# Depthwise convolution and token mixer: DMA transposes against TensorE transposes with packed matmul tiles and a static schedule

## Chip, cores and metric

The kernel runs on one core of a Trainium2 chip. The metric is the device time of one execution in microseconds (us); smaller is better. In this text PE is TensorE, DVE is VectorE, ACT is ScalarE, POOL is GpSimd and SP is SyncE. A matmul has a stationary operand, which a weight load (PEld) brings into PE, and a moving operand. The time from the start of one matmul to the start of the next grows with the columns of the moving operand (192 columns 83 ns, 512 columns 216 ns in the trace of before, so 2.4 columns per ns); that time is called streaming here. The programs write the results to PSUM, which they use in banks. To evacuate a result is to copy it out of PSUM with DVE or ACT. Two small stationary operands can share the array (in the trace of after both of such a pair start 0 to 5 ns apart): side by side they are called column tiles here, one above the other row tiles. A landing is the end of a DMA transfer.

## The reference, cut to what matters

```python
# x: (8, 4224, 192) float32; weight: (8, 7); w_q, w_k: (192, 64); w_out: (192, 192)
w = softmax(weight)                       # one 7-tap filter for each of 8 heads of 24 channels
x = causal_conv(x, w)                     # out[s] = sum_k w[k] * x[s - 6 + k], per channel
wq = x @ w_q;  wk = x @ w_k
W_tok = (1 / 8) * einsum('bsd,btd->bst', wq, wk)
mixed = einsum('bst,btd->bsd', W_tok, x)
out = maximum(mixed, 0) @ w_out           # (8, 4224, 192) float32
```

No softmax stands between the two products, so both kernels reorder them. They form the Gram matrix G = xᵀx of the convolved x once per batch and compute `relu(x @ (scale * w_q w_kᵀ G)) @ w_out`. A convolution over 128 tokens is a product with a 128×128 band matrix, of which 122 outputs are valid. Both programs make G from x with tokens on the partitions and run the second pass on x with channels on the partitions, so one of the two forms is made by transposing.

## The kernel before

The convolution puts channels on the partitions, with 24-column tiles of the array. DVE copies the result to `XT`. SyncE then transposes it with the DMA engines to `XS`, in five pieces per batch and two transposes per piece, and the Gram products run when all of it has landed.

```python
# gen_conv_block: four chunks of 122 tokens, four heads side by side in the array
last = te.matmul(
    tile[32 * g : 32 * g + GRP, CW * ci : CW * ci + ncol],
    XW[0:kc, xbuf, c, GRP * h : GRP * h + GRP],
    BAND[0:kc, h, 0:ncol],
    start=True, stop=True,
    tile_position=(0, 32 * g),
)
# ... DVE: XT <- tile ...
# gen_transpose_piece
for t in range(2):
    sy.dma_start_transpose(
        XS[:, xbuf, i0 : i0 + nchunk, 128 * t : 128 * t + 128],
        XT[:, xbuf, t, s0 : s0 + plen],
    ).then_inc(ch.sem, 16)
# gen_g_chunk: 33 chunks a batch, 2 x 256 columns each
te.matmul(P_G0[:, 0:256], XS[:, xbuf, i, 0:128], xall, start=first, stop=last)
mm = te.matmul(P_G1[:, 0:256], XS[:, xbuf, i, 128:256], xall, start=first, stop=last)
# ... M = wkᵀ G, A = wq M (192 x 192) ...
# gen_mx_quad: four 128x128 matmuls of 512 columns
last = te.matmul(P_MX[m][:, 0:ncols], A_SB[:, tt, 128 * m : 128 * m + 128],
                 XT[:, xbuf, tt, s0 : s0 + ncols], start=(tt == 0), stop=(tt == 1))
# ... ACT: RT <- relu; gen_final: two matmuls of 192 columns per 128 tokens ...
# stores from POOL: a row of 192 floats (768 bytes) per token
dst = bass.AP(out_t, (b * S + jstart * 128) * D, [[D, 128], [128 * D, nsubs], [1, D]])
```

Of the kernel before, what the change touches and what calls it, by code (L numbers as in the profile page):

```python
# [9 lines left out]
F32 = mybir.dt.float32  # L10


def bass_lightweight_conv__then__hypermixer_token_mlp_kernel(
# [12 lines left out]
    assert S % 128 == 0 and S >= 1024  # L26
    assert D == 192 and H == 8 and KC == 7 and DH == 64 and GRP == 24

    x_t = x.tensor
    out_t = out.tensor  # L30
    w_t = weight.tensor
    wq_t = moe_w_q.tensor
    wk_t = moe_w_k.tensor
    wo_t = moe_w_out.tensor

    CW = 122
    NCC = (S + CW - 1) // CW
    NBLOCK = (NCC + 3) // 4
    NQT = (S + 511) // 512
    NSUB = S // 128  # L40
    NCH = S // 128
    PIECES = []
    c0 = 0
    for size in (8, 8, 8, 6, 100):
        if c0 >= NCH:
            break
        PIECES.append(list(range(c0, min(c0 + size, NCH))))
        c0 += size
    NPIECE = len(PIECES)
    scale = 1.0 / (float(DH) ** 0.5)  # L50

    es = contextlib.ExitStack()
    es.__enter__()

# [3 lines left out]
    def psum(name):  # L58
        return es.enter_context(nc.psum_tensor(name, [128, 512], F32))

    class Chan:
        def __init__(self, name):
            self.sem = es.enter_context(nc.semaphore(name))
            self.v = 0

        def inc(self, n=1):
            self.v += n
            return self.v

    c_wsetup = Chan("c_wsetup")  # L70
    c_xload = [[Chan(f"c_xl{xb}_{i}") for i in range(3)] for xb in range(2)]
    c_spdma = Chan("c_spdma")
    c_tp = [[Chan(f"c_tp{xb}_{p}") for p in range(NPIECE)] for xb in range(2)]
    c_odma = [Chan("c_odma0"), Chan("c_odma1")]
    c_dve = Chan("c_dve")
    c_act = Chan("c_act")
    c_gp = Chan("c_gp")
    c_convA = Chan("c_convA")
    c_convB = Chan("c_convB")
    c_evA = Chan("c_evA")  # L80
    c_evB = Chan("c_evB")
    c_gd = Chan("c_gd")
    c_ge = Chan("c_ge")
    c_md = Chan("c_md")
    c_me = Chan("c_me")
    c_ad = Chan("c_ad")
    c_ae = Chan("c_ae")
    c_mxd = Chan("c_mxd")
    c_mxe = Chan("c_mxe")
    c_fd = Chan("c_fd")  # L90
    c_fe = [Chan("c_fe_dve"), Chan("c_fe_act")]

    WT_F = sbuf("wt_f", [128, H * KC], F32)
    WMX = sbuf("wmx", [128, H], F32)
    WEX = sbuf("wex", [128, H, KC], F32)
    WSM = sbuf("wsm", [128, H], F32)
    WSOFT = sbuf("wsoft", [128, H, KC], F32)
    DMASK = sbuf("dmask", [128, KC, 128], F32)
    BANDF = sbuf("bandf", [128, 128], F32)
    BAND = sbuf("band", [128, H, 128], BF16)  # L100
    IDENT_T = sbuf("ident_t", [128, 128], F32)
    IDENT = sbuf("ident", [128, 128], BF16)
    WQP = sbuf("wqp", [128, 2, DH], BF16)
    WQT = sbuf("wqt", [DH, 2, 128], BF16)
    WKP = sbuf("wkp", [128, 2, DH], BF16)
    WOP = sbuf("wop", [128, 2, D], BF16)
    XW = sbuf("xw", [128, 2, NCC, D], BF16)
    XT = sbuf("xt", [128, 2, 2, S], BF16)
    XS = sbuf("xs", [128, 2, NCH, 256], BF16)
    G_SB = sbuf("g_sb", [128, 2, 256], BF16)  # L110
    M_SB = sbuf("m_sb", [DH, 256], BF16)
    A_SB = sbuf("a_sb", [128, 2, 256], BF16)
    RT = sbuf("rt", [128, 2, 2, 512], BF16)
    OUT_SB = sbuf("out_sb", [128, 2, 8, D], F32)

    P_CONVA = psum("p_conva")
    P_CONVB = psum("p_convb")
    P_G0 = psum("p_g0")
    P_G1 = psum("p_g1")
    P_M = psum("p_m")  # L120
    P_MX0 = psum("p_mx0")
    P_MX1 = psum("p_mx1")
    P_A = psum("p_a")
    P_OUTS = [P_G0, P_G1]
    P_MX = [P_MX0, P_MX1]

    conv_mm_ch = [c_convA, c_convB]
    conv_ev_ch = [c_evA, c_evB]
    conv_tile = [P_CONVA, P_CONVB]

    streams = {"pe": [], "act": [], "dve": [], "sp": [], "pool": []}

    def pe(f):
        streams["pe"].append(f)

    def act(f):
        streams["act"].append(f)

    def dve(f):
        streams["dve"].append(f)  # L140

    def sp(f):
        streams["sp"].append(f)

    def pool(f):
        streams["pool"].append(f)

    def waiter(eng, waits):
        for s, v in waits:
            if v > 0:  # L150
                eng.wait_ge(s, v)

    def _setup_sp(sy):
        src = bass.AP(w_t, 0, [[0, 128], [1, H * KC]])
        sy.dma_start(WT_F[:, :], src).then_inc(c_spdma.sem, 16)

    sp(_setup_sp)
    v_wtf = c_spdma.inc(16)

    def _setup_pool_mem(gp):  # L160
        gp.memset(WQP[:, :, :], 0.0).then_inc(c_gp.sem, 1)
        gp.memset(WKP[:, :, :], 0.0).then_inc(c_gp.sem, 1)
        gp.memset(WOP[:, :, :], 0.0).then_inc(c_gp.sem, 1)
        gp.memset(XW[0:6, :, 0, :], 0.0).then_inc(c_gp.sem, 1)

    pool(_setup_pool_mem)
    v_gp_mem = c_gp.inc(4)

    def _setup_pool_dma(gp, v_mem=v_gp_mem):
        gp.wait_ge(c_gp.sem, v_mem)  # L170
        for t in range(2):
            for g in range(4):
                d0 = 96 * t + 24 * g
                gp.dma_start(
                    WQP[32 * g : 32 * g + 24, t, :],
                    bass.AP(wq_t, d0 * DH, [[DH, 24], [1, DH]]),
                ).then_inc(c_wsetup.sem, 16)
                gp.dma_start(
                    WKP[32 * g : 32 * g + 24, t, :],
                    bass.AP(wk_t, d0 * DH, [[DH, 24], [1, DH]]),  # L180
                ).then_inc(c_wsetup.sem, 16)
                gp.dma_start(
                    WOP[32 * g : 32 * g + 24, t, :],
                    bass.AP(wo_t, d0 * D, [[D, 24], [1, D]]),
                ).then_inc(c_wsetup.sem, 16)

    v_wload = None

    v_mx = c_dve.inc(1)
    v_sub = c_dve.inc(H)  # L190

    def _setup_dve_softmax(ve, v_wtf=v_wtf, v_mx=v_mx):
        wt3 = WT_F[:, :].rearrange("p (h k) -> p h k", k=KC)
        ve.wait_ge(c_spdma.sem, v_wtf)
        ve.tensor_reduce(WMX[:, :], wt3, AX.X, ALU.max).then_inc(c_dve.sem, 1)
        ve.wait_ge(c_dve.sem, v_mx)
        for h in range(H):
            ve.tensor_scalar(
                WEX[:, h, :], wt3[:, h, :], WMX[:, h : h + 1], None,
                op0=ALU.subtract,  # L200
            ).then_inc(c_dve.sem, 1)

    dve(_setup_dve_softmax)

    def _setup_act_exp(sc, v_sub=v_sub):
        sc.wait_ge(c_dve.sem, v_sub)
        sc.activation(WEX[:, :, :], WEX[:, :, :], AF.Exp).then_inc(c_act.sem, 1)

# [142 lines left out]
    def piece_chunks(p):  # L351
        return PIECES[p]

# [512 lines left out]
```

## Time and profile before

| | before |
|---|---|
| time, median of 3 runs | 378.26 us (377.14 to 381.84) |
| PE / DVE / ACT busy | 66% / 40% / 31% of the span |
| chain that ended last | PE 35%, DMA 23%, SyncE's queue 17% |

The page gives for each engine its busy time, and in its second part the busy share in 40 equal slices (each digit is tenths). "Chain that ended last" follows the last instruction back to what released it. From the page of the kernel before: PE's total, its slices, and the chain by engine and by line.

```profile
PE 247.1 (66%) x3618; PEld 158.0 (42%) x3618; DVE 149.5 (40%) x301; ACT 116.6 (31%) x244; POOL 84.7 (23%) x123
...
PE   0001447479586958796769868975789297959671
...
PE 35%; DMA 23%; SPq 17%; DVE 13%; issue 5%; ACT 5%; POOL 0%; DVEq 0%; POOLq 0%
SPq L479 17%; DMA xs<-xt 12%; PE p_mx L584 11%; DMA out_dram<-out_sb 10%; PE p_conva L437 6%; PE p_g L501 5%; DVE xt L460 5%; DVE bandf L281 5%; PE p_g L502 4%; PE p_g L622 3%; ACT rt L603 3%; PE p_g L624 2%; PE p_convb L437 2%; DVE out_sb 
```

PE is never full for long, and SyncE, which only issues transfers in this program, holds 17% of the chain: it issues the transposes (L479). The same chain in order of time shows how one batch waits. Columns are start in us, duration in us, and what held the chain.

```profile
177.27 3.29 SPq L479
...
180.66 2.58 SPq L479
...
183.28 8.23 DMA xs<-xt
...
191.55 0.28 PE p_g L501
```

In this batch the transposes are issued one after another, the last four for 2.6 to 3.7 us each. The last one takes 8.23 us to land, and only then do the Gram products (L501) start.

PE's records overlap: a Gram matmul of 256 columns lasts 0.27 us, and the next one starts 0.11 us after it. What one matmul costs is therefore read from the start of one to the start of the next. From the timeline of the kernel before (start, duration, engine, line, operation, rows*columns of the stationary operand, moving operand, count):

```profile
160.82 1.04 PE L584 MATMUL p_mx<-xt,a_sb 128*128 128x512 bf16 x4
161.79 0.39 PE L437 MATMUL p_conva<-band,xw 128*24 128x122 bf16 x16
162.01 0.39 PE L437 MATMUL p_convb<-band,xw 128*24 128x122 bf16 x16
```

Four matmuls with a stationary operand of 128*128 take 4 × 215 ns = 0.86 us by the interval found elsewhere in this trace (512 columns, 215 to 216 ns). The next group, of another form (128*24), starts after 0.97 us. So 0.11 us went to the change of form.

### The profile page before, as it was taken

To read this page: it belongs to the slowest core of one execution; us is meant where nothing else is said; L and a number is where in the kernel's file an instruction comes from. 1 tells how busy PE (TensorE), PEld (TensorE's weight loads), DVE (VectorE), ACT (ScalarE), POOL (GpSimd) and SP (SyncE) were. 2 spreads that over 40 slices of the span, in tenths; PEclk is the share of its full clock that TensorE was granted. 3 is DMA by queue.
4 is the path that set the end of the run, shared out by engine and by line. 5 is a ranking of instruction groups with operands and counts; after the bars stand their busy time and mean duration, and the time that the engine had idled before them with its cause. 6 is when DMAs were issued, how large, how long until landed. Compare 5 with 4: busy or idle time off the path is not lost.

```text
span 376.1 us, 8598 instructions
## 1 busy us (share of the span) xinstructions
PE 247.1 (66%) x3618; PEld 158.0 (42%) x3618; DVE 149.5 (40%) x301; ACT 116.6 (31%) x244; POOL 84.7 (23%) x123
## 2 busy tenths in 40 slices
PE   0001447479586958796769868975789297959671
PEld 0001225245363636463645446544555174536341
DVE  5997440057304730474036513651266106710121
ACT  1000000046403740375016511661166104630561
POOL 8980004001240115012500150015001100120021
PEclk9999999699789996999689969996999689988998
DMA  1990079948999799999996999699949934893055
GB/s 12 184 179 4 2 108 153 151 31 179 251 197 123 174 248 189 141 176 247 207 129 93 233 255 177 104 238 249 169 78 197 226 91 57 193 224 107 2 167 178
DMA packets 114229, 57.57 MB, mean 153 GB/s; under 512 B 108304, under 2 KB 108432, under 8 KB 114192
## 3 DMA queue, kind: packets, MB, share of 16 engines
q0 software_dynamic: 43904, 39.69, 54.6%
q1 hardware_dynamic: 70288, 17.34, 35.1%
q8 instruction: 29, 0.48, 0.5%
q14 instruction: 8, 0.07, 0.1%
HBM read 27.48 MB, written 25.95 MB: 142 GB/s over the span
## 4 chain that ended last, share of the span: by engine, by line
PE 35%; DMA 23%; SPq 17%; DVE 13%; issue 5%; ACT 5%; POOL 0%; DVEq 0%; POOLq 0%
SPq L479 17%; DMA xs<-xt 12%; PE p_mx L584 11%; DMA out_dram<-out_sb 10%; PE p_conva L437 6%; PE p_g L501 5%; DVE xt L460 5%; DVE bandf L281 5%; PE p_g L502 4%; PE p_g L622 3%; ACT rt L603 3%; PE p_g L624 2%; PE p_convb L437 2%; DVE out_sb L639 1%; DVE bandf L276 1%
## 5 line engine op out<-in xcount | busy, mean ns | idle before, releaser
L501 PE MATMUL p_g<-xs 128*128 128x256 bf16 x264 | 76.2, 322 | 31.7 <-DVE out_sb L639 17.4
L460 DVE CAST xt<-p_conva 128x488 bf16<-128x488 f32 (+1 forms) x72 | 46.5, 645 | 120.6 <-PE p_conva L437 120.5
L667 POOL DMA_DIRECT2D out_dram<-out_sb x40 | 33.2, 829 | 256.0 <-DVE out_sb L639 169.4
L603 ACT ACTIVATE rt<-p_mx 128x512 bf16<-128x512 f32 x144 | 73.1, 560 | 39.8 <-PE p_mx L584 39.7
L584 PE MATMUL p_mx<-xt,a_sb 128*128 128x512 bf16 (+1 forms) x288 | 69.4, 363 | 16.4 <-ACT rt L603 14.4
L502 PE MATMUL p_g<-xs 128*128 128x256 bf16 x264 | 75.9, 322 | 0.0
L639 DVE COPY out_sb<-p_g 128x384 f32<-128x384 f32 (+1 forms) x72 | 38.2, 530 | 78.9 <-DMA out_dram<-out_sb 46.5
L622 PE MATMUL p_g<-wop,rt 128*128 128x192 bf16 x264 | 50.5, 250 | 19.0 <-ACT rt L603 14.5
L437 PE MATMUL p_conva<-band,xw 128*24 128x122 bf16 (+1 forms) x1120 | 30.0, 231 | 44.2 <-DVE band L287 22.2
L460 DVE CAST xt<-p_convb 128x488 bf16<-128x488 f32 (+1 forms) x72 | 46.0, 639 | 15.1 <-PE p_convb L437 15.1
L624 PE MATMUL p_g<-wop,rt 128*128 128x192 bf16 x264 | 50.4, 249 | 0.0
L501 PEld LDWEIGHTS p_g<-xs 128*128 128x128 bf16 x264 | 30.3, 115 | 43.5 <-issue 19.3
L437 PEld LDWEIGHTS p_conva<-band,xw 128*24 128x24 bf16 (+1 forms) x1120 | 17.5, 96 | 66.9 <-issue 66.9
L646 ACT COPY out_sb<-p_g 128x384 f32<-128x384 f32 x64 | 30.7, 480 | 31.3 <-DMA out_dram<-out_sb 18.1
L584 PEld LDWEIGHTS p_mx<-xt,a_sb 128*128 128x128 bf16 x288 | 21.6, 97 | 42.6 <-ACT rt L603 20.8
L517 ACT CAST g_sb<-p_g 128x256 bf16<-128x256 f32 x8 | 3.0, 372 | 112.0 <-PE p_g L502 112.0
L622 PEld LDWEIGHTS p_g<-wop,rt 128*128 128x128 bf16 x264 | 25.8, 98 | 27.9 <-ACT rt L603 16.1
L437 PE MATMUL p_convb<-band,xw 128*24 128x122 bf16 (+1 forms) x1120 | 29.4, 228 | 6.2 <-DVE xt L460 6.2
L502 PEld LDWEIGHTS p_g<-xs 128*128 128x128 bf16 x264 | 30.1, 114 | 7.5
L624 PEld LDWEIGHTS p_g<-wop,rt 128*128 128x128 bf16 x264 | 26.0, 98 | 1.7
L387 POOL DMA_DIRECT2D xw<-in_x_dram x24 | 25.9, 1089 | 0.0
L437 PEld LDWEIGHTS p_convb<-band,xw 128*24 128x24 bf16 (+1 forms) x1120 | 18.6, 97 | 12.7 <-DVE xt L460 8.3
(47 smaller groups left out, 82.5 us busy)
## 6 DMA issues: line engine op xcount, KB each, us to landing
out_dram<-out_sb POOLq DMA_DIRECT2D x32, 768.0 KB, 6.2
xw<-in_x_dram POOLq DMA_DIRECT2D x24, 528.0 KB, 10.8
xs<-xt SPq DMA_TRANSPOSE x80, 6.6
out_dram<-out_sb POOLq DMA_DIRECT2D x8, 96.0 KB, 4.8
xw<-in_x_dram POOLq DMA_DIRECT2D x8, 45.8 KB, 4.9
xw<-in_x_dram POOLq DMA_DIRECT2D x8, 30.8 KB, 11.9
wqp<-in_moe_w_q_dram POOLq DMA_DIRECT2D x8, 3.0 KB, 9.7
wkp<-in_moe_w_k_dram POOLq DMA_DIRECT2D x8, 3.0 KB, 9.4
```

The lines of the kernel that those rows point to most:

```text
L437: last = te.matmul(tile[32 * g : 32 * g + GRP, CW * ci : CW * ci + ncol], XW[0:kc, xbuf, c, GRP * h : GRP * h + GRP], BAND[0:kc, h, 0:ncol ...
L460: ve.tensor_copy(XT[:, xbuf, hg, c0 : c0 + ncols], tile[:, 0:ncols]).then_inc(ch.sem, 1)
L479: sy.dma_start_transpose(XS[:, xbuf, i0 : i0 + nchunk, 128 * t : 128 * t + 128], XT[:, xbuf, t, s0 : s0 + plen],).then_inc(ch.sem, 16)
L501: te.matmul(P_G0[:, 0:256], XS[:, xbuf, i, 0:128], xall, start=first, stop=last)
L502: mm = te.matmul(P_G1[:, 0:256], XS[:, xbuf, i, 128:256], xall, start=first, stop=last)
L584: last = te.matmul(P_MX[m][:, 0:ncols], A_SB[:, tt, 128 * m : 128 * m + 128], XT[:, xbuf, tt, s0 : s0 + ncols], start=(tt == 0), stop=(tt ...
L603: sc.activation(RT[:, rbuf, m, 0:ncols], P_MX[m][:, 0:ncols], AF.Relu, scale=scale).then_inc(c_mxe.sem, 1)
L622: te.matmul(pout[0:128, col : col + D], RT[:, rbuf, 0, 128 * u : 128 * u + 128], WOP[:, 0, :], start=True, stop=False)
L624: te.matmul(pout[0:128, col : col + D], RT[:, rbuf, 1, 128 * u : 128 * u + 128], WOP[:, 1, :], start=False, stop=True).then_inc(c_fd.sem, 1)
L639: ve.tensor_copy(OUT_SB[:, slot, j0 % 8 : j0 % 8 + n, :], pout[0:128, 0 : n * D].rearrange("p (x d) -> p x d", d=D),).then_inc(c_fe[0].sem, 1)
L646: sc.copy(OUT_SB[:, slot, j0 % 8 : j0 % 8 + n, :], pout[0:128, 0 : n * D].rearrange("p (x d) -> p x d", d=D),).then_inc(c_fe[1].sem, 1)
L667: gp.dma_start(dst, OUT_SB[:, slot, 0:nsubs, :]).then_inc(c_odma[slot].sem, 16)
```

## The change

The intent is to take the DMA transposes out of the loop and then keep PE busy. The convolution now gives tokens on the partitions, which is the Gram operand as it stands. The channel form for the second pass is made by 432 PE transposes. The 192×192 matrix A is replaced by a rank-64 pair of steps (Q, then Z), in which the two halves of a batch (2112 tokens each) are packed side by side in the array. Four tokens share one 3072-byte output row. The program keeps all of x in SBUF, so all its loads run ahead. A greedy planner fixes the order of all jobs before the program is built, with one fixed PE time per job.

The diff, cut to its core (most of both files differs; cuts are marked):

```diff
-                    last = te.matmul(
-                        tile[32 * g : 32 * g + GRP, CW * ci : CW * ci + ncol],
-                        XW[0:kc, xbuf, c, GRP * h : GRP * h + GRP],
-                        BAND[0:kc, h, 0:ncol],
-                        start=True, stop=True,
-                        tile_position=(0, 32 * g),
-                    )
+                last = e.matmul(PS[:, k + j, 0:432], BAND[:, h, :], rhs, start=True, stop=True)
 ...
-                sy.dma_start_transpose(
-                    XS[:, xbuf, i0 : i0 + nchunk, 128 * t : 128 * t + 128],
-                    XT[:, xbuf, t, s0 : s0 + plen],
-                ).then_inc(ch.sem, 16)
+                    last = e.transpose(
+                        bank[:, s_ * sec + o0 : s_ * sec + o0 + m], src, IDENT[0:m, 0:m]
+                    )
 ...
+    def job_q(b, k):                      # two halves of the batch in two column tiles
+            e.matmul(o[0:64], WQ1[:, :], y[:, 0], start=True, stop=False, skip_group_check=True)
+            e.matmul(o[64:128], WQ1[:, :], y[:, 1], start=True, stop=False,
+                     skip_group_check=True)
+            e.matmul(o[0:64], WQ2[0:64], y[0:64, 2], start=False, stop=True,
+                     skip_group_check=True)
+            return e.matmul(o[64:128], WQ2[64:128], y[64:128, 2], start=False, stop=True,
+                            skip_group_check=True)
 ...
+            # job_g: Gram, three matmuls a chunk, 192 + 192 + 128 columns
+            e.matmul(PS[:, 7, 0:192], y[:, 0:128], y[:, 0:192], start=c == 0, **fl)
+            e.matmul(PS[:, 7, 192:384], y[:, 256:384], y[:, 192:384], start=False, **fl)
+            return e.matmul(
+                PS[:, 7, 384:512], y[:, 128:256], y[:, 128:256], start=False, **fl
+            )
 ...
+            for h in range(2):            # job_zd: two row tiles of 64; job_zs likewise, 64 columns
+                r = slice(64 * h, 64 * h + 64)
+                last = e.matmul(PS[:, bk + h, 0:w], M_SB[r, b % 2, 0:128],
+                                QT[r, b % 2, s0 : s0 + w], start=True, stop=True)
 ...
+            for h in range(2):            # job_o: four full matmuls, then four in row tiles
+                for j in range(2):
+                    r = 2 * q + j
+                    e.matmul(PS[:, bk + h, 192 * j : 192 * j + 192], ZT[:, zr, h, r::4],
+                             WO1[:, :], start=j == 0, stop=False, **kw)
+            for j in range(2):
+                for h in range(2):
+                    r = 2 * q + j
+                    hs = slice(64 * h, 64 * h + 64)
+                    last = e.matmul(PS[:, bk + h, 192 * j : 192 * j + 192],
+                                    ZT[hs, zr, 2, r::4], WO2[hs, :], start=False, stop=j == 1,
+                                    **kw)
 ...
+        t = free["pe"] if job.pe else 0.0 # planner: no term for a change of form
+        if job.banks == 2:
+            t = max(t, min(s[1] for s in doubles) + 0.12)
+        elif job.banks == 1:
+            t = max(t, single[0][1] + 0.12)
```

PSUM is cut into three double banks (convolution, transposes, ZD, output), one single bank (Q, ZS and small products) and one bank for G.

## The prediction

> **What bounds the kernel now.** No engine is full: the page shows PE busy 66% of 376.1 us, VectorE 40%, ScalarE 31%. The chain of waits that ended last gives PE only 35%, and DMA 23% plus the SyncE queue that issues transposes 17%. In order of time, each batch has 10 to 17 us of transposes issued one after another and an 8 to 9 us landing; then the Gram products run alone (66 matmuls, 107 ns apart: 7 us) while ScalarE waits (112 us in all). Building the bands takes 34 us (22 to the first conv), and the last second pass runs alone (about 18 us). The limit is a serial loop of about 39 us per batch, not throughput.
>
> **What the change does.**
> - Removes 80 DMA transposes: 35% of 16 DMA engines' span (132 us of packet time) and the long pole.
> - Conv result is token-major, so it is the Gram operand as it stands.
> - Adds 432 TensorE transposes and their evacuation; replaces A by Q plus Z (64-row tiles, in pairs).
> - Stores 3072-byte rows, x loads all run ahead; one static order.
>
> **Costs of the new loop, all batches.** Matmul intervals from the timeline: 512 columns 215 ns, 256 in 107, 192 in 83, so 2.4 columns/ns[...].
> PE: conv 128 x 180 ns = 23; [...]Q 14 if its column tiles overlap (the old conv's 16 tiled matmuls in 0.22 us show they do); Gram 31-34; Z 14 if paired; output 32; small products 3: about 150. [...]0.06-0.09 us at a switch between conv and full matmuls. Some 40 switches per batch: about 20-28 us more. PE 170-178.
> Evacuation: VectorE 0.157 us + 1.04 ns/column, ScalarE 0.12-0.17 + 0.83. With the program's counts: ScalarE about 125-133, VectorE about 133-140 if the bf16 transposes go at half cost[...].
> DMA: x loaded at 190 GB/s early (13.7 MB: 72 us), stores 330 GB/s when alone (26 MB: 79 us): about 150.
> So four resources lie between 125 and 178 us, PE ahead.
>
> **Critical path.** Start to first conv about 10 us, PE loop about 165-168[...], in-order queues and PSUM hand-overs[...] 5-12, last evacuation and store landing (3-4.5 us in this trace) 5.
>
> **Predicted: 188 us**, 8 in 10 within 172 to 206. Faster by over 2%: 0.985; within 2%: 0.01; slower: 0.005.
>
> **What would show it.** PE at 85% busy or more, weight loads with it, in the middle slices; the chain of waits mostly PE, SPq gone, DMA only at ends; [...]gaps of 0.05-0.1 us where tiling mode changes; VectorE and ScalarE 65-80%; DMA full in the first 100 us, lighter later; first conv near 10 us.
>
> **What would make it wrong.** Slower: row tiles not overlapping (+20 us), Q serial (+14), slow strided weight loads for the output (+10), [...]VectorE not at double rate on transposes (+24 on it), stores waiting on x loads, the static order misfitting real durations.[...]

PE was put at about 150 us without changes of form. The terms printed come to 117 to 120 us; the rest, about 30 us, was the term for the 432 PE transposes. (For Gram, 144 chunks of 512 columns are 30.7 us at 2.4 columns per ns; what the upper end of 31-34 adds is not worked out.) With 20-28 us for changes of form PE came to 170-178 us. The critical path was 10 + 165-168 + 5-12 + 5 = 185 to 195 us, recorded as 188. Its PE loop is 5 to 10 us shorter than 170-178, because the author assumed that part of the cost of changes hides, which no trace showed. (In the trace of before ACT starts 0.20 us and DVE 0.22 us, in the median, after the columns of the matmul that they waited for would end at 2.4 per ns; PE starts 0.06 us after the end of an ACT evacuation that it waited for, and 0.15 us after one of DVE.) The half cost of the bf16 transposes on VectorE was the author's assumption; only the trace of after shows it (732 columns in 533 ns). The 0.06-0.09 us at a switch is a reading by eye; the 138 changes of the trace of before give 0.098 us in the mean.

## The result, and the profile after

| | before | after |
|---|---|---|
| time, median of 6 runs each | 378.22 us (373.05 to 384.7) | 223.75 us (222.89 to 225.81) |
| ratio of fast runs | | 0.5951, 95% interval 0.59 to 0.6002 |
| PE / DVE / ACT busy | 66% / 40% / 31% | 91% / 58% / 56% |

A ratio here is the mean time of one kernel's fast runs over that of the other's fast runs of the same rounds, so it is not quite the ratio of the medians.

The change is a large gain, 155 us, but the time lies 36 us above the predicted 188 us and above the range. From the page of the kernel after, the lines that answer to those of before:

```profile
PE 202.6 (91%) x1936; PEld 119.3 (53%) x1936; DVE 129.6 (58%) x226; ACT 125.4 (56%) x231; POOL 48.8 (22%) x80
...
PE   7548999999999999999999999999999999776870
...
PEclk9965999999999999999999999999999999999697
...
PE 81%; DMA 6%; DVE 4%; POOL 4%; ACT 2%; issue 1%; ACTq 0%
PE ps L439 12%; PE ps L604 11%; PE ps L387 11%; PE ps L493 8%; PE ps L610 8%; PE ps L469 5%; PE ps L472 5%; PE ps L494 5%; PE ps L585 5%; PE ps L564 4%; DMA out_dram<-o_sb 4%; PE ps L495 3%; DMA xw<-in_x_dram 3%; POOL xw L191 2%; DVE zt L75
```

SyncE's queue is gone from the chain, and PE holds 81% of it. The slices show PE at 9 tenths nearly throughout, at the full granted clock. The windows view adds up busy time by stretch (columns: PE, PE weight loads, DVE, ACT, POOL, each with instruction counts; then granted clock, DMA share and GB/s):

```profile
30.00:180.00 150.00, 149.69 (x1503) 89.86 (x1501) 96.08 (x164) 96.88 (x184) 23.82 (x33) 1.00 0.92 198
180.00:224.00 44.00, 30.53 (x301) 17.76 (x299) 16.97 (x26) 19.46 (x28) 0.00 (x0) 0.93 0.39 148
```

From 30 to 180 us PE is busy 149.69 of 150 us. The kernel is bound by PE there, as predicted, so the missing 36 us must be more PE time than was counted, plus something at the two ends. "Busy" does not say what PE did. The timeline does:

```profile
100.29 0.39 PE L469 MATMUL ps<-yt,wq 128*64 128x488 bf16 x1
100.29 0.39 PE L470 MATMUL ps<-yt,wq 128*64 128x488 bf16 x1
100.61 0.39 PE L472 MATMUL ps<-yt,wq 64*64 64x488 bf16 x1
...
100.94 0.26 PE L493 MATMUL ps<-y 122*128 122x192 bf16 x1
101.03 0.25 PE L494 MATMUL ps<-y 122*128 122x192 bf16 x1
```

The two column tiles start together, so they overlap as intended. Their 488 columns stream in 203 ns at 2.4 columns per ns (in this trace too 192 columns start 82 to 83 ns and 512 columns 216 ns before the next). But the next pair, which has 64 rows in place of 128, starts 0.32 us later, and the Gram product after it another 0.32 us later. Each of these two steps is about 120 ns longer than its columns, and nothing was waited for: no "idle before" stands on these lines. Between two Gram products of the same form (100.94 to 101.03) there is no such surplus: 192 columns need 80 ns.

I did this arithmetic for all matmuls of the trace. For each start-to-start interval I subtracted the columns over 2.4. I then sorted the rest by whether the stationary operand's form changed, where "form" is its rows and columns, each rounded up to 32, 64 or 128. A surplus over 60 ns with the same form counts as a wait. At a change with a surplus over 160 ns, all beyond 100 ns counts as a wait. The sorting assumes the full clock, so streaming at half clock is booked as a wait too: that is 3.4 of the 13.6 us of waits below (2.0 us before 30 us, 1.4 us after 190 us).

| term | in the prediction's sum | in the trace of after |
|---|---|---|
| start to the first convolution | about 10 | 14.4 |
| columns streamed, plus surpluses of up to 60 ns within a form | about 150 | 138.9 + 8.7 = 147.6 |
| changes of form | 15 to 18 (the rest of 165 to 168) | 42.0, in 405 changes |
| PE waits | 5 to 12 | 13.6, of which 9.7 after 190 us |
| after the last matmul | 5 | 5.8 |
| sum | 185 to 195, recorded as 188 | 223.4 of a span of 223.6 |

By kind, in means: leaving a full 128×128 form, or a 64×128 form, costs 92 to 98 ns; leaving a 64×64 form costs 111 to 118 ns, and going from 128×64 to 64×64 costs 119 ns. Leaving 128×64 for the full form costs only 98 ns in the eight cases here. The last Gram chunk of a batch half has 38 tokens, and even that counts: going from 122 rows to 38 costs 98 ns and going back 91 to 96 ns.

The two ends show on the timeline as well. At the start (PE and DVE lines; the bracket is the idle time before and who ended it):

```profile
13.05 0.43 DVE L311 TENSOR_TENSOR tmp<-tmp 128x304 bf16<-128x304 bf16 x1
...
14.44 3.06 PE L387 MATMUL ps<-xw,band 128*128 128x432 bf16 x8 [5.61 <-ACT band L322]
18.28 0.54 PE L387 MATMUL ps<-xw,band 128*128 128x432 bf16 x1 [0.78 <-DMA xw<-in_x_dram]
```

The first convolution waited for the band matrix until 14.44 us, and the next group of it waited until 18.28 us for x. At the end, in the last batch:

```profile
195.19 0.60 ACT L748 ACTIVATE zt<-ps 128x512 bf16<-128x512 f32 x1 [0.50 <-PE ps L585]
...
195.84 0.52 PE L604 MATMUL ps<-wo,zt 128*128 128x192 bf16 x4 [0.69 <-ACT zt L748]
```

A matmul of the output waits 0.69 us for the evacuation of a Z tile, which itself waited for a Z matmul. With no other batch left to fill in, this ping-pong is exposed.

The theory to test is therefore: **each change of form costs a fixed 0.1 us or so of PE time that nothing hides, and the prediction counted too few of them at too low a price.** The rivals were: (a) the surplus is the weight load of the next form and grows with columns or depends on operands; (b) the time is really hand-overs of PSUM between engines under the static order, and would come back as waits if the changes went; (c) a lower clock, against which the granted clock of 1.00 in the windows above speaks already; (d) most of the 36 us are start and end.

### The profile page after: what moved, and what is told of

The parts are those of the page before. It is cut to its first block, busy times and chain, and to the rows that moved or that the text cites. A ratio compares the mean times of both kernels' runs of the same rounds, so it can differ in the third digit from the quotient of the medians.

```text
span 223.6 us, 4628 instructions
## 1 busy us (share of the span) xinstructions
PE 202.6 (91%) x1936; PEld 119.3 (53%) x1936; DVE 129.6 (58%) x226; ACT 125.4 (56%) x231; POOL 48.8 (22%) x80
## 3 DMA queue, kind: packets, MB, share of 16 engines
q0 software_dynamic: 36480, 13.63, 51.6%
q1 hardware_dynamic: 11040, 26.31, 32.2%
## 4 chain that ended last, share of the span: by engine, by line
PE 81%; DMA 6%; DVE 4%; POOL 4%; ACT 2%; issue 1%; ACTq 0%
PE ps L439 12%; PE ps L604 11%; PE ps L387 11%; PE ps L493 8%; PE ps L610 8%; PE ps L469 5%; PE ps L472 5%; PE ps L494 5%; PE ps L585 5%; PE ps L564 4%; DMA out_dram<-o_sb 4%; PE ps L495 3%; DMA xw<-in_x_dram 3%; POOL xw L191 2%; DVE zt L750 2%; DVE o_sb L745 1%
## 5 line engine op out<-in xcount | busy, mean ns | idle before, releaser
L745 ACT COPY o_sb<-ps 128x768 f32<-128x768 f32 (+1 forms) x51 | 37.3, 734 | 28.0 <-PE ps L610 24.8
L745 ACT CAST y<-ps 128x432 bf16<-128x432 f32 (+2 forms) x89 | 36.3, 474 | 18.2 <-PE ps L387 17.4
L745 DVE COPY yt<-ps 128x732 bf16<-128x732 bf16 (+1 forms) x66 | 31.7, 530 | 16.9 <-PE ps L439 16.6
L387 PE MATMUL ps<-xw,band 128*128 128x432 bf16 x128 | 33.9, 369 | 6.7 <-ACT band L322 5.6
L745 DVE CAST y<-ps 128x432 bf16<-128x432 f32 (+2 forms) x55 | 29.3, 578 | 17.0 <-PE ps L387 16.6
L604 PE MATMUL ps<-wo,zt 128*128 128x192 bf16 x256 | 33.4, 254 | 3.9 <-DVE zt L750 2.5
L750 DVE TENSOR_SCALAR zt<-ps 128x512 bf16<-128x512 f32 (+3 forms) x42 | 31.5, 766 | 8.6 <-PE ps L564 6.6
L493 PE MATMUL ps<-y 122*128 122x192 bf16 x144 | 34.9, 252 | 0.0
L494 PE MATMUL ps<-y 122*128 122x192 bf16 x144 | 34.1, 246 | 0.0
L495 PE MATMUL ps<-y 122*128 122x128 bf16 x144 | 31.6, 219 | 0.0
L439 PE MATMUL ps<-ident,y 122*128 122x122 bf16 (+1 forms) x432 | 29.5, 220 | 0.0
L745 ACT CAST qt<-ps 128x488 bf16<-128x488 f32 (+1 forms) x27 | 14.5, 536 | 13.7 <-PE ps L474 13.5
L493 PEld LDWEIGHTS ps<-y 122*128 122x128 bf16 x144 | 13.9, 97 | 14.4 <-issue 11.5
```

The costliest lines, as they stand in the source:

```text
L387: last = e.matmul(PS[:, k + j, 0:432], BAND[:, h, :], rhs, start=True, stop=True)
L439: last = e.transpose(bank[:, s_ * sec + o0 : s_ * sec + o0 + m], src, IDENT[0:m, 0:m])
L493: e.matmul(PS[:, 7, 0:192], y[:, 0:128], y[:, 0:192], start=c == 0, **fl)
L494: e.matmul(PS[:, 7, 192:384], y[:, 256:384], y[:, 192:384], start=False, **fl)
L495: return e.matmul(PS[:, 7, 384:512], y[:, 128:256], y[:, 128:256], start=False, **fl)
L604: e.matmul(PS[:, bk + h, 192 * j : 192 * j + 192], ZT[:, zr, h, r::4], WO1[:, :], start=j == 0, stop=False, **kw)
```

## Experiments

Eighteen kernels ran, in five groups; kernels of one group ran on one chip beside the kernel before. "Changes" are counted in the program, costs are worked out from the trace as above, and "waits" are PE waits from 30 to 170 us unless said otherwise. All results are correct except where a kernel is wrong. The unedited kernel ran as ctrl in the first group only. The later groups ran on other chips, where the mean of the fast runs of the kernel before lies between 371.5 and 374.2 us, against 376.6 us beside ctrl. A difference of 1 or 2% against ctrl is therefore not clear of the chip, and the ratios can give another size than the times do; where it matters, both are given. The first group (before: 378.09 us median) is ctrl, q2_wide, o_alternate and o_full.

### ctrl: the kernel after, unedited

> The changed kernel again, unedited, as the base for the three others on this chip. Every theory expects 223 to 226 us.

Measured: 225.35 us (223.59 to 226.88), ratio 0.5986 [0.5933, 0.6039]. 405 changes, 41.9 us; waits 0.5 us. It is the base for its group.

### q2_wide: one change of form fewer in each Q job

```diff
-            e.matmul(o[0:64], WQ2[0:64], y[0:64, 2], start=False, stop=True,
+            e.matmul(o[0:64], WQ2P[:, 0, :], y[:, 2], start=False, stop=True,
                      skip_group_check=True)
-            return e.matmul(o[64:128], WQ2[64:128], y[64:128, 2], start=False, stop=True,
+            return e.matmul(o[64:128], WQ2P[:, 1, :], y[:, 2], start=False, stop=True,
                             skip_group_check=True)
```

`WQ2P` is WQ2 padded with zeros to 128 rows, so the second pair has the form of the first. The streamed columns are the same.

> The second pair of Q products uses all 128 rows with zero-padded weights, so the 40 changes from 128 rows by 64 columns to 64 by 64 inside the Q jobs are gone; streamed columns, evacuations and order are the same. Theory D (a change of tiling form costs PE about 0.10 to 0.12 us, nothing else about it matters): 40 x 0.12 = 4 to 5 us less, so 219 to 220 us, and the first Q pair followed by the second after about 205 ns instead of 323. Theory W (PE is held by evacuation and PSUM banks, its busy time only looks full): unchanged within 1 us. Theory F (64-wide matmuls are slow in themselves): unchanged, still 64 columns wide.

Measured: 219.94 us (219.41 to 220.91), ratio 0.5846 [0.5811, 0.5882]; 5.4 us less than ctrl; 40 changes fewer at 0.12 us make 4.8. In its trace all changes together cost 36.4 us, 5.5 less, because leaving the Q pair for the full form has also become cheaper (98 ns, where leaving 64×64 cost 118). From its timeline on PE:

```profile
98.38 0.39 PE L472 MATMUL ps<-yt,wq 128*64 128x488 bf16 x1
98.38 0.39 PE L473 MATMUL ps<-yt,wq 128*64 128x488 bf16 x1
98.61 0.37 PE L475 MATMUL ps<-yt,wq2p 128*64 128x488 bf16 x1
...
98.91 0.26 PE L496 MATMUL ps<-y 122*128 122x192 bf16 x1
```

The second pair now starts 0.23 us after the first, not 0.32 us, with the same columns in each. The step out of Q takes 0.30 us, because the form still changes there. More work in the array (more rows) took less time.

### o_alternate: more changes, the same matmuls

```diff
-            for h in range(2):
-                for j in range(2):
+            for j in range(2):
+                for h in range(2):
                     r = 2 * q + j
                     e.matmul(PS[:, bk + h, 192 * j : 192 * j + 192], ZT[:, zr, h, r::4],
                              WO1[:, :], start=j == 0, stop=False, **kw)
-            for j in range(2):
                 for h in range(2):
```

The eight matmuls of an output job run 2, 2, 2, 2 instead of 4, 4: 533 changes instead of 405.

> The same eight matmuls of an output job, reordered: two of 128 rows, two of 64, two of 128, two of 64, so 128 more changes of tiling form in all, with the same columns streamed, the same evacuations and the same job order. Theory D: 128 x 0.10 = about 13 us more, so 236 to 238 us. Theory F: unchanged, as the matmuls are the same. Theory W: unchanged within 2 us.

Measured: 246.65 us (246.18 to 247.2), ratio 0.6558 [0.6517, 0.66]; 21.3 us more, where 13 had been expected. Timelines on PE, first of ctrl, then of o_alternate:

```profile
117.91 0.49 PE L604 MATMUL ps<-wo,zt 128*128 128x192 bf16 x4
...
118.63 0.52 PE L604 MATMUL ps<-wo,zt 128*128 128x192 bf16 x4
```

```profile
122.08 0.33 PE L604 MATMUL ps<-wo,zt 128*128 128x192 bf16 x2
...
122.55 0.36 PE L604 MATMUL ps<-wo,zt 128*128 128x192 bf16 x2
...
123.05 0.36 PE L604 MATMUL ps<-wo,zt 128*128 128x192 bf16 x2
```

The same eight matmuls take 0.72 us in ctrl and 0.97 us here, so two more changes cost 0.25 us. Of this, 23 to 27 ns per pair of full matmuls lie between its two members (110 ns from start to start, where 83 to 87 ns are usual); why was not tested. The kernel after has the same 110 ns in output jobs, in 39 of the 42 places where the first of two full matmuls stands right behind a change, so it goes with the change, though the sorting above books it as a surplus within a form. The rest lies at the changes themselves. In the middle a batch is 2.0 us longer, 16 us in all. The other 5 us or so come at the end, where the last batch takes 23.4 us instead of 16.3 us with the clock lowered. The row of granted clock in the page of o_alternate shows it:

```profile
PEclk9979999999999999999999999999999999555555
```

The last six slices stand at half clock. So 13 us was right in kind, low in price for this case, and the end is a separate loss whose reason (why the clock fell just here) I did not test; after 190 us, streaming at half clock takes about 6 us more than in ctrl.

### o_full: changes against columns

```diff
-                                    ZT[hs, zr, 2, r::4], WO2[hs, :], start=False, stop=j == 1,
+                                    ZT[:, zr, 2, r::4], WO2P[:, h, :], start=False, stop=j == 1,
```

The row-tiled half of the output job is padded to full matmuls, which no longer run in pairs.

> The 64-row pairs of the output jobs become full 128-row matmuls on zero-padded weights: about 128 changes of form fewer (13 us less) but 128 x 83 ns = 10.6 us more streaming, as the pairs no longer overlap. Theory D: the two nearly cancel, 220 to 223 us. A theory in which form changes are free: 10 us slower, 233 to 236 us. Theory W: unchanged within 2 us.

Measured: 224.81 us (223.71 to 225.37), ratio 0.5969 [0.5932, 0.6006], the same as ctrl. There are 315 changes, 90 fewer (the expectation had counted about 128); they cost 33.4 us, 8.5 less. The unpaired columns add about 10 us (64 jobs × 2 × 80 ns). Gain and loss cancel, so packing into row tiles is worth nothing here once its changes are paid.

### probe: the price by itself

The second group (before: 373.85 us median) is probe, all_full, start and tail. The probe adds chains of matmuls on an otherwise idle PE: same form, or alternating full with row, column or quarter tiles, at 64, 192 and 448 columns. The rest of the kernel is untouched.

```diff
+        for n in (64, 192, 448):
+            for i in range(6):
+                last = full(n)
+            for i in range(6):
+                last = rowh(n, 0)
+            for i in range(5):
+                last = full(n)
+                last = rowh(n, 0)
+            # ... likewise full with a 128x64 and a 64x64 operand
```

> Measures the disputed cost alone: after the 24 warming matmuls, while PE would wait for the bands, chains on zeroed data for 64, 192 and 448 streamed columns: six of full form, six of 64 rows, then full alternating with 64 rows, with 64 columns, and with 64 by 64. Theory D: same form follows same form after columns / 2.4 ns (about 30, 83, 189 ns); each change adds a constant of about 0.09 to 0.12 us whatever the number of columns, and more when a 64-column form is left than when the full one is. A theory in which the gap is a weight load that isn't hidden: the added time shrinks as the streamed columns before it grow, and at 448 columns (187 ns of streaming) it is gone.

Measured: one run, 251.0 us, state unknown; only the intervals inside count. Timeline on PE at 64 columns, then at 448 columns:

```profile
8.75 0.20 PE L362 MATMUL ps<-warm 128*128 128x64 bf16 x1
8.88 0.20 PE L363 MATMUL ps<-warm 64*128 64x64 bf16 x1
9.01 0.20 PE L362 MATMUL ps<-warm 128*128 128x64 bf16 x1
...
28.53 0.56 PE L362 MATMUL ps<-warm 128*128 128x448 bf16 x1
29.02 0.55 PE L363 MATMUL ps<-warm 64*128 64x448 bf16 x1
```

| columns | clock | same form | full to row | row to full | 128×64 to full |
|---|---|---|---|---|---|
| 64 | full | 29 ns | 135 to 136 (+106 to 107) | 131 to 133 (+102 to 104) | 149 (+120) |
| 192 | half | 160 ns | 275 (+115) | 272 (+112) | 302 (+142) |
| 448 | half | 373 ns | 488 (+115) | 485 (+112) | 515 (+142) |

The surplus is the same at 192 and 448 columns, both at half clock, and chains of one form, which load weights just as often, do not have it. So it is not an ordinary load that a longer stream would hide, which rules out rival (a). What PE does in that time these runs do not show. Nothing else ran in these chains, so it is no hand-over. The clock fell to half within the probe, which was not planned; the surplus rose there by about a tenth to a fifth, not twofold. In the probe one 128×64 tile stands alone and leaving it costs 120 ns; in q2_wide, where two stand side by side, leaving them costs 98 ns. So the form that is left does not set the price alone; what does was not tested.

### all_full: nearly no changes, more columns

Everything is padded to 128×128: Q becomes three full matmuls, ZD two unpaired ones, ZS one with a block-diagonal operand, and O as in o_full. Its core:

```diff
+            for i in range(3):
+                last = e.matmul(o, WQF[:, i, :], y[:, i], start=i == 0, stop=i == 2,
+                                skip_group_check=True)
+            return last
 ...
-                last = e.matmul(PS[:, bk + h, 0:w], M_SB[r, b % 2, 0:128],
-                                QT[r, b % 2, s0 : s0 + w], start=True, stop=True)
+                last = e.matmul(PS[:, bk + h, 0:w], M_DF[:, b % 2, h, :],
+                                QT[:, b % 2, s0 : s0 + w], start=True, stop=True)
```

> All products in the full 128 by 128 form on zero-padded operands (Q in three matmuls, both Z, output), same order of jobs. From the per-form intervals: streaming grows by about 7 us in Q, 7 us in Z and 10.6 us in the output jobs (25 us in all), and some 300 to 330 of the 405 changes of form vanish (31 to 34 us at 0.104 us). Theory D: 6 to 11 us faster than the changed kernel, 213 to 219 us. If changes of form were free: 20 us slower or more, about 245 us.

Measured: 224.91 us (223.42 to 225.67), ratio 0.6044 [0.5993, 0.6095]: no gain, where 213 to 219 had been expected. The 77 changes cost 7.7 us, 34 less. Counted from the program at 2.4 columns per ns, the unpaired columns add about 24 us (O 10, Q 7, ZD 7). The balance of 10 us went into waits, which rose from 0.5 to about 12 us (11 matmul records are missing from that window, at 0.21 us each worth up to 2.3 us of it). The windows view shows PE no longer full:

```profile
30.00:180.00 150.00, 142.58 (x1442) 108.18 (x1453) 99.39 (x175) 97.26 (x193) 27.19 (x37) 0.98 0.94 201
```

PE is busy 142.58 of 150 us, where after had 149.69. Some 2.9 us of the waits are not waiting but streaming at half clock; the granted clock is 0.98 in this window. This was the first sign that rival (b) is not all wrong: with the changes gone, a second limit came close behind.

### start: the beginning

```diff
-    load(0, 0, 0, 1, xg[0][0], [z_first])
-    load(0, 0, 1, 8, xg[0][0])
-    load(0, 1, 0, 9, xg[0][1])
     # ... masks on POOL ...
+    load(0, 0, 0, 1, xg[0][0], [z_first])
+    load(0, 0, 1, 8, xg[0][0])
+    load(0, 1, 0, 9, xg[0][1])
-        for i in range(24):
+        for i in range(33):
```

POOL makes the masks of the band matrix before it issues the first loads, and the warm-up is longer.

> Only the start is changed: GpSimd makes the masks before it issues the loads of x, VectorE clears the six first rows before the large clear, and 33 warming matmuls instead of 24. The first conv should come at 10 to 11 us instead of 14.4, the second group of chunks should no longer wait until 18.3, and the granted clock of the first 30 us should rise from 0.72-1.00. Theory (start-up is a serial prefix): 4 to 6 us faster, 218 to 220 us. Rival (a later resource catches up with it, such as x loading): unchanged.

Measured: 224.28 us (223.59 to 224.34), ratio 0.6027 [0.5985, 0.607], against an expected gain of 4 to 6 us. The first convolution began at 12.6 instead of 14.4 us but now waited for x. The second group began at 16.96 instead of 18.28 us, again after waiting for x. So the trace gains about 1.3 us (span 222.6 us against 223.9 in ctrl): the band matrix was only the last of two waits, and the load of x lies just behind it. The run times of start and ctrl overlap, and the ratio of start is no lower than that of ctrl, so as a gain in time this is not shown.

### tail: the end

```diff
+    def ones(job):
+        last = ("GEV", B - 1) in done
+        return single + (doubles + [gbank] if last else [])
-            t = max(t, single[0][1] + 0.12)
+            t = max(t, min(s[1] for s in ones(job)) + 0.12)
```

After the last Gram, jobs that need one bank may take any free one.

> After the last Gram result is out, Q, Z's 64-wide part and the small products may take any free PSUM bank instead of the one single bank. Theory (the last 30 us wait for one bank, in series): waits of PE after 190 us fall from about 10 us to 5 and the time by 4 to 6 us, 218 to 220 us. Rival (the end is a chain of data, output after Z after Q): unchanged within 2 us.

Measured: 216.89 us (216.49 to 217.2), ratio 0.5832 [0.5781, 0.5882], 8.5 us less than ctrl by the times; the ratios of the two, 0.5832 and 0.5986, would make it 5.8 us. In its trace, waits after 190 us fall from 9.6 to 1.3 us and the last batch takes 9.2 us instead of 16.3. The middle is unchanged (waits 0.4 us). So rival (d) holds in part: some 6 to 8 us of the kernel's time lie in the single bank at the end and about 1 us at the start. Not all of that is part of the missing 36 us, as the prediction's sum already held 5 to 12 us of waits.

### replan, combo, combo_b, full_replan: a planner that knows the price

The third group (before: 372.06 us median) gives the planner the measured PE times and a cost for a change of form:

```diff
-        t = free["pe"] if job.pe else 0.0
+        t = free["pe"] + (0.1 if job.forms[0] != form[0] else 0.0) if job.pe else 0.0
-            key = (max(t, free["pe"] + 0.03), pr)
+            lost = 0.05 if streams[s][head[s]].pe and streams[s][head[s]].forms[0] != form[0] else 0.0
+            key = (max(t, free["pe"] + 0.03) + lost, pr)
```

replan has the same matmuls as after, plus the free banks of tail.

> Every matmul, evacuation and transfer of the changed kernel, in another static order: the planner that fixes it is given the measured durations and 0.1 us for each change of form, and the end may use any free bank as in the run called tail. Counted in the program: 345 changes of form instead of 405. Theory D: 60 x 0.104 = 6 us less in the steady part and 8 us less at the end, as tail showed, so 209 to 213 us. Rival (the order only moves waits about): no faster than the run called tail, 217 us.

combo adds to such a planner (with `lost` 0.02, another order of priorities, and any free bank for single-bank jobs throughout) the edits of q2_wide and start, and makes ZS one matmul with a block-diagonal operand:

```diff
-            for h in range(2):
-                r = slice(64 * h, 64 * h + 64)
-                last = e.matmul(PS[r, bk, 0:w], M_SB[r, b % 2, 128:192],
-                                QT[r, b % 2, s0 : s0 + w], start=True, stop=True)
-            return last
+            return e.matmul(PS[:, bk, 0:w], M_BD[:, b % 2, :],
+                            QT[:, b % 2, s0 : s0 + w], start=True, stop=True)
```

> All that helped, with a plan that avoids changes of form: second Q products on 128 rows, the 64-wide part of Z as one full matmul on a block-diagonal operand, the reordered start, free banks for the small jobs, and other priorities. Streamed columns hardly change; the program has 216 changes of form instead of 405. Theory D: 189 x 0.104 = 20 us less, 8 us at the end, 1 us at the start: 194 to 198 us, if PE stays the bound. If evacuation or x loading becomes the bound, waits of PE in the middle grow from 0.5 us to 5 or 10 and the time is 200 to 206 us.

combo_b differs from combo in priorities and `lost` (0.05), and frees the other banks only at the end.

> The same matmuls and evacuations as in combo under another priority list, with 275 changes of form in the program, 59 more. Theory D: about 6 us slower than combo in PE's own time. If combo is held by other waits, the two come out within 2 us.

full_replan is all_full with the new planner (`lost` 0), the edit of start and the free banks of combo.

> All products in full form as in the run called all_full, which gained nothing although its PE work is less: its waits inside the middle part were 13 us against 0.5. Here the order is planned for the full forms, with the start and end of combo; 73 changes of form. Theory (all_full's relief was lost to an order planned for other durations): PE's own time is about 180 us, so 200 to 206 us. Rival (evacuation is then the bound, whatever the order): 213 us or more, with VectorE and ScalarE waiting little.

| | time, us | ratio [95%] | changes, their cost in us | waits, us |
|---|---|---|---|---|
| replan | 225.44 (225.03 to 226.35) | 0.6077 [0.6052, 0.6101] | 345, 35.9 | 14.5 |
| combo | 205.93 (205.92 to 207.75) | 0.556 [0.5526, 0.5594] | 216, 21.1 | 11.2 |
| combo_b | 216.68 (215.97 to 218.11) | 0.5842 [0.5805, 0.5879] | 275, 27.0 | 12.1 |
| full_replan | 221.56 (218.91 to 223.53) | 0.5934 [0.5866, 0.6002] | 73, 7.3 | 10.8 |

One of the four runs of full_replan (223.53 us) was slow; its ratio leaves it out. replan and full_replan miss their expectation by 12 us or more. combo took the second branch of its expectation (200 to 206 us, with waits). combo_b is 10.8 us slower than combo, where about 6 had been expected: its changes cost 5.9 us more, as expected, and its waits after 190 us are 4.0 us longer. In replan the changes cost 6 us less and the waits 14 us more. Its windows line:

```profile
30.00:180.00 150.00, 138.02 (x1399) 85.26 (x1398) 77.74 (x147) 95.88 (x176) 24.00 (x33) 1.00 0.87 183
```

PE is busy 138.02 us here against 149.69, and DVE only 77.74 against 96.08. Its PE waits are for Z tiles (10.3 us), spread over the whole window. Fewer changes mean longer runs of one kind of job, and the new order spaced the evacuations worse; which rule of the planner does it I did not separate. A planner with truer prices gave a worse program, so price alone does not make a good order.

### additive: the repairs without the new planner

The fourth group (before: 378.43 us median). Edits of q2_wide, start, tail and the one-matmul ZS, with the original planner.

> The four single edits together, with the changed kernel's own order and planner figures: second Q products on 128 rows, the 64-wide part of Z as one full matmul, free banks at the end, the reordered start. The program has 324 changes of form (405 before). Theory D with the parts measured so far: 81 x 0.104 = 8.4 us less, 8 us at the end, 1 us at the start: 206 to 209 us. If the parts share one cause, such as waits that only move, 213 us or more.

Measured: 207.69 us (207.34 to 207.72), ratio 0.5548 [0.55, 0.5596], as expected. 324 changes cost 31.8 us; waits are 3.0 us. Gains of parts add up while waits stay small. Against combo: combo has 108 fewer changes, worth 11 us, and is only 2 us faster in its median and not at all by the ratios (0.556 against 0.5548, on different chips), because its waits are 8 us longer.

### no_changes and no_changes_tail: the whole price at once

Their outputs are wrong, which doesn't matter for the times. All matmuls of the loop have the full form, but the streamed columns stay those of after: Q, ZD and O compute on fewer columns or products than a right result in full form would need.

```diff
-                last = e.matmul(PS[:, bk + h, 0:w], M_SB[r, b % 2, 0:128],
-                                QT[r, b % 2, s0 : s0 + w], start=True, stop=True)
+                last = e.matmul(PS[:, bk + h, 0 : w // 2], M_SB[:, b % 2, 0:128],
+                                QT[:, b % 2, s0 : s0 + w // 2], start=True, stop=True)
```

> Wrong result on purpose. Every pair of 64-row or 64-column matmuls that run together becomes one full matmul of the same columns (in Z two of half the columns), so that PE streams the same 139 us while the program has 79 changes of form instead of 405; evacuations, transfers, job order, start and end stay, but for five writes of PSUM at the start and three small evacuations of M instead of one. Theory D: up to 326 x 0.104 = 34 us less, 190 us, if nothing else binds; if evacuation or hand-overs take over as in all_full, waits of PE in the middle grow and it is 195 to 210 us. If changes of form are free: 224 us.

Measured: 203.01 us median (200.11 to 206.61; fast runs 200.11 and 202.34), ratio 0.5378 [0.5265, 0.549]. Two of the four runs are slow. There are 79 changes, 7.9 us, so 34 us of changes are gone; by the fast runs (mean 201.2 us, against 223.75 of the kernel after and 225.35 of ctrl) 22 to 24 us came back.

> Wrong result on purpose. The same with the start and the end repaired as in the runs start and tail. Theory D: 9 us less than no_changes; with all three mis-sized terms gone the prediction's own sum, 188 us, should come out within some 8 us. If it stays above 200 us, a further term was missed, and it is waits for evacuation.

no_changes_tail adds the edits of start and tail. Measured: fast runs 188.61 and 187.02 us, two more at 193.18 and 194.14 us over 1.5% above the fastest, so no interval. That is the time predicted. But its terms are not the predicted ones: changes are 8 us where 15 to 18 had been counted, and waits are 8.8 us in the middle.

Of the 10.6 us of waits in no_changes (0.5 in ctrl), 10.3 lie in one place. Windows of after, then of no_changes:

```profile
30.00:110.00 80.00, 79.69 (x809) 48.39 (x807) 51.12 (x89) 51.58 (x100) 23.82 (x33) 1.00 1.39 248
110.00:170.00 60.00, 60.00 (x600) 35.73 (x598) 39.13 (x65) 39.12 (x71) 0.00 (x0) 1.00 0.35 131
```

```profile
30.00:110.00 80.00, 71.23 (x725) 54.01 (x726) 51.02 (x89) 51.03 (x109) 25.43 (x34) 0.94 1.41 251
110.00:170.00 60.00, 60.00 (x668) 47.87 (x666) 45.57 (x79) 45.97 (x91) 0.00 (x0) 1.00 0.45 166
```

Up to 110 us, while x is still being loaded, PE is busy 71.23 of 80 us; afterwards it is busy 60.00 of 60. The timeline on ACT at the longest of its waits:

```profile
97.58 0.32 ACT L745 COPY o_sb<-ps 128x192 f32<-128x192 f32 x1 [3.87 <-DMA out_dram<-o_sb]
```

ACT stood 3.87 us because an earlier store had not left the output buffer. Three such waits sum to 8.7 us. Meanwhile ACT evacuates nothing, so PSUM stays full and PE waits. PE's own waits in no_changes from 30 to 170 us (what PE waited for: us in total, times, longest):

```profile
PE ps L395 <- ACT o_sb L745: 4.7, 2, 3.2
PE ps L395 <- DMA xw<-in_x_dram: 2.5, 1, 2.5
PE ps L478 <- ACT qt L745: 2.0, 1, 2.0
```

The first and the third line, 6.7 us, lie behind the three waits for a store: each ends with the evacuation that had waited, or with the one that ACT did right after it. The second line, a landing of x, began before 30 us and is not in the 10.3 us. Some 2.7 of the 10.3 us are not waiting but streaming at half clock: the granted clock fell to 0.94 in the first window. A store of 768 KB takes 9.2 us from issue to landing (median) between 60 and 95 us and 4.6 us between 110 and 150 us. (The DMA share in these lines exceeds 1, so I draw nothing from its size.)

### no_changes_paced, combo_paced, additive_paced: loads that do not run ahead

The fifth group (before: 377.18 us median) asks whether those late stores come from the x loads that run ahead on the same DMA engines (the page counts the queues of both on the core's 16 engines: in the trace of after the packets of the loads' queue took 51.6% of their span, those of the stores' queue 32.2%). The loads of batch b now wait for the last convolution of batch b-3.

```diff
+            if job.name[0] == "Y" and job.name[2:] == (1, 3) and job.name[1] + 3 < B:
+                load_batch(job.name[1] + 3, [pop])
```

> Wrong on purpose, as no_changes was. The one edit beside that run: the loads of batch b wait until the last convolution of batch b-3, instead of all running ahead. In no_changes the matmul engine stood about 10 us between 30 and 110 us and 0.2 us between 110 and 170 us; ScalarE stood 8.7 us in three waits for the landing of an output store, in the time when loads and stores share the DMA engines. Theory 'loads that run ahead delay the stores': the waits of the matmul engine in 30 to 110 us fall to under 4 us and the kernel takes 194 to 198 us (no_changes: fast runs 200.1 and 202.3). Rival 'evacuation by VectorE and ScalarE is the next limit': time unchanged within 2 us, waits still about 10 us, now spread over 30 to 170 us.

> Correct. Combo with the same pacing. In combo the matmul engine stood 10.2 us in 30 to 110 us and 1.0 us after it, and six waits of ScalarE for an output store summed to 9.0 us. Theory 'loads that run ahead delay the stores': 196 to 201 us (combo: 205.9). Rival: 205 to 207.

> Correct. Additive with the same pacing. There the matmul engine stood only 3.0 us in 30 to 110 us, so both theories expect little: 204.5 to 207.5 us (additive: 207.7). If this gains more than 4 us, the pacing does something else than take away those waits.

| | time, us | ratio [95%] | waits in 30 to 110 us: paced (not paced) | ACT waits for a store: paced (not paced) |
|---|---|---|---|---|
| no_changes_paced (wrong) | 201.39 (200.43 to 202.79) | 0.5344 [0.53, 0.5387] | 10.3 (10.3) | 10.2 (8.7) |
| combo_paced | 201.41 (199.94 to 201.52) | 0.5344 [0.5304, 0.5384] | 7.5 (10.2) | 2.3 (9.0) |
| additive_paced | 206.01 (205.54 to 206.48) | 0.5475 [0.544, 0.551] | 2.6 (3.0) | 1.8 (5.3) |

(In each of the three paced traces 15 matmul records of 512 columns are missing, 6 or 7 of them in 30 to 110 us. At 0.21 us each, up to 1.5 us of the paced waits in that window is not real.) For combo the theory mostly holds: its waits for stores fall from 9.0 to 2.3 us, and 4.5 us come off its median (8 us by the ratios, on different chips), where 5 to 10 had been expected. The control gains 1.7 us, as expected. For no_changes the theory failed: time and waits stay. There the same kinds of wait remain, up to 3.8 us long. Perhaps pacing by three batches moves the loads too little in the first 100 us; that was not tested. So that late stores are the link is read from the waits; that the loads cause them is supported in combo and not in no_changes, and it stays open there. combo_paced is the fastest correct kernel, 0.9 of the kernel after by the medians (201.41 against 223.75).

## Why the prediction was right or wrong

**What bounds the kernel before: right.** The chain of waits named the serial loop of transposes, landing and Gram. When it was removed, SyncE vanished from the chain and the time fell by 41%.

**PE becomes the limit: right.** 85% busy or more was predicted; it is 91%, and 149.69 of 150 us in the middle.

**Columns streamed: right, with errors inside.** About 150 us was predicted and 147.6 us measured. The transposes, of 122 columns, start 53 to 54 ns apart, 23 us in all, where the recorded sum held about 30 us or more for them. The trace of before had a nearer price than the one used: its full-form matmuls of 128 columns (L584) start 55 to 66 ns apart. Column tiles of Q and row tiles of Z overlap; both of a pair start 3 to 4 ns apart in the median. The strided weight loads of the output are not slow (81 to 88 ns a matmul within a form, and 105 to 115 ns in 39 of the 42 places right behind a change).

**Evacuation: right in time, wrong in share.** DVE and ACT have 129.6 and 125.4 us of work, against predictions of 133 to 140 and 125 to 133. DVE copies 732 bf16 columns from PSUM in 533 ns, 0.51 ns a column after 0.157 us, half of the 1.04 ns that it takes for float32 (384 columns in 552 ns in the trace of before). Their shares are 58 and 56%, not 65 to 80%, because the span is longer.

**Changes of form: the step that failed.** The prediction put it as "Some 40 switches per batch: about 20-28 us more", at 0.06 to 0.09 us each, and then let part of it go: "PE loop about 165-168", on the assumption that some of it hides. That a change costs PE time was right and the size was wrong, in three factors. The program has 51 changes per batch, 405 in all. Each costs 0.104 us on average. And none hides: PE was already full, so each is a gap in the critical engine. The term measures 42.0 us where 15 to 18 us had been left in the sum, 24 to 27 of the 36 us missing. Adding changes (o_alternate), removing them (q2_wide) and the probe all show the price. Taking nearly all of them out gave back 22 to 24 us, not 34, since some 10 us of other waits took their place; 6.7 of them are read as late stores.

The numbers were to be had beforehand. The count can be made from the program text. The price lies in the trace of before: the same arithmetic finds 138 changes there and 13.5 us, 0.098 each (all but one between 92 and 100 ns, so the 0.06 to 0.09 us of the prediction was a misreading). I had read it off three spots by eye.

**Start: too low.** About 10 us was predicted, 14.4 measured. In the trace of the edited start only about 1 us of this comes back, because the load of x lies right behind.

**Waits and end: a little low.** 5 to 12 us was predicted, 13.6 measured, of which 9.7 in the last batch; the tail edit takes 6 to 8 us out. The prediction had named "the static order misfitting real durations" as a danger but had put no number to the last batch, where nothing is left to fill in.

**The range** (172 to 206) was to allow for dearer changes of form as well, but gave this no more room than one of many risks, though it was the least well measured term of the sum.

## What to carry to other kernels

When small tiles are packed into PE, count every change of the stationary operand's form in instruction order and charge it at its measured start-to-start surplus, about 0.1 us here; on the full PE of this case none of it hid, and padding a small operand with zeros to its neighbour's form can be the faster choice (in q2_wide by 5.4 us). A busy share near 100% does not show this loss: subtract the streamed columns from the intervals between starts. When one limit is taken away, look at once for the next (here late output stores and the last batch's PSUM banks), since gains stop adding up when waits return.
